# First K in fp32 by SyncE's queue, first Q by GpSimd's, two late stores by GpSimd's queue, and a redrawn order, in an attention and SiLU feed-forward kernel

## The chip, the core and the metric

The kernel runs on one core of a Trainium2 chip. The core has TensorE (matrix products, PE in the profile, with its weight loads as PEld), VectorE (DVE), ScalarE (ACT), GpSimd (POOL) and SyncE (SP), which all run at the same time and wait for each other by semaphores. SP, ACT and POOL also issue DMA transfers. The metric is the device time of one execution in microseconds (us); lower is better. The time before is a median of 384.25 us over three runs (383.94 to 386.96).

## The reference, cut to what matters

Inputs are fp32. Attention over 8 batches, 12 heads, 448 tokens and head dimension 64 gives the input of a feed-forward block with 3584 rows, width 768 and inner width 2048:

```python
scores = scale * np.matmul(q, k.transpose(0, 1, 3, 2))
scores = scores - np.max(scores, axis=-1, keepdims=True)
attn = np.exp(scores)
attn = attn / (np.sum(attn, axis=-1, keepdims=True) + 1e-09)
x = np.matmul(attn, v)            # then transposed and reshaped to (3584, 768)
h = x @ w_in
g = h * (1.0 / (1.0 + np.exp(-h)))
out = g @ w_out
```

## The kernel before, in words

**Work and tiles.** One unit of attention is one batch and a group of four heads (a "head group", three of them per batch). The first batch is cut once more into two pieces of 224 queries, so that units 0 to 2 and then 3 to 5 are the two pieces of its three head groups. All matmuls take fp16. For a unit, K and Q are loaded as [128 partitions, 14 tokens x 64], turned by VectorE (`turn_k` and `turn_q`, L411 and L422), multiplied on TensorE (`score`, L430), put through the exponential on ScalarE (`expo`, L469), summed (L510, L524), multiplied by V (L495) and scaled on VectorE into the rows of x (`norm`, L634). The feed-forward layers follow: the first (L647, and L783 for the last two pairs of batches), its SiLU (L668, L693, L829), the second (L864, and L877 for the first four output tiles), and VectorE or ScalarE collect the results in fp32 tiles called `ost`, from which `store` (L902 to L914) writes 32 rows at a time to memory.

**Loads.** Nearly all loads are DMAs of GpSimd's queue, because they turn fp32 in memory into fp16 on the way. There is one exception before the change: the first 448 columns of Q of unit 0 come in fp32 through SyncE's queue into a borrowed tile (`first_q`, L340 to L344) and ScalarE casts them to fp16 (`cast_q`, L347). The order of the other loads is a string, `LOADS`: `u` is K and Q of a unit, `v` is V, `i` a quarter of the first layer's weights, `o` a quarter of the second's.

**Stores.** Each `ost` tile of 128 x 384 leaves in four DMAs. The outputs come in 14 groups (`qd`, 0 to 13) of 256 rows, four tiles to a group. All four DMAs of a tile go through SyncE's queue, except in groups 12 and 13, where two of the four go through ScalarE's queue. Group 13 ends with tile (0, 1) and then tile (0, 0), of which VectorE copies one half and ScalarE the other (L929, L930).

**Order.** The order on every engine is not written by hand. When the program is built, a planner (`Order`, `Op`, and the loop at the end of the function) plays the work through with assumed costs and due times and emits the instructions in the order that comes out. Its constants (`NEAR`, `LATE`, `WHOLE`, the `_B` biases, `TURN`, `SOON`, `HOLD`, `DMA_PAUSES`, `FIRST_Q`) decide which of two ready pieces goes first. Where the planner sees TensorE without work in the first part, it inserts matmuls of a zero tile (`run_zeros`, L1815) that keep the engine running; the first of these blocks has at least 5120 columns. In the second half TensorE uses two ways of placing a product: whole 128 x 128 weights, or four strips of 32 columns side by side (`strips`). Changing between these and the four row strips of the scores is called a switch below.

**The end.** After its last instruction each engine executes a DRAIN and takes part in a barrier (L1922), after SyncE has waited for the landing of every DMA.

Of the kernel before, what the change touches and what calls it, by code (L numbers as in the profile page):

```python
# [9 lines left out]
FP16 = mybir.dt.float16  # L10
# [8 lines left out]
HOP = 0.10  # L19
DMA_ROW = 0.004  # L20
DMA_RATE = 13400.0
FIRST_Q = 3.5
DMA_PAUSES = ((0.0, 0.4), (4.0, 1.35), (15.5, 0.9), (21.0, 0.7), (48.5, 0.8), (65.0, 0.8))
LANES = 8
LANE = 0.28
FETCH = 5.6
# [9 lines left out]
def act(n):  # L36
    return n * 0.000824 + 0.177
# [61 lines left out]
class Order:  # L99


    def __init__(self, shy, nice):
# [3 lines left out]
        self.pool = []  # L106
        self.dma_free, self.loads, self.pauses = 0.0, [], list(DMA_PAUSES)
        self.pe_n, self.fetched = 0, 0.0
# [112 lines left out]
def kernel(  # L221
# [9 lines left out]
    nc = tc.nc  # L231

    B, NH, S, D = q.shape
# [3 lines left out]
    NG = NH // HG  # L237
    TPP = S // 32
# [9 lines left out]
    NT = 2 * S // 128  # L248
    OH = DM // 2
    NRK, NRQ = 3, 4  # L250
# [3 lines left out]
    EAGER = 1  # L254
    PAIRS = (B - 4, B - 2)
    LAST = {B - 4: range(DFF // 256), B - 2: range(DFF // 256)}
    NEAR = 0.1
    LATE = -2.0
    COLD = 8.5
    FIRST = 40  # L260
    WHOLE = 7
    TANH_B = -1
    GATE_B = -6
    ADD_B = 1
    SUM_B = -3
    COPY_B = -1
    READ_B = -2
    PAIR_B = -2
    SILU_B = -2
    HOLD = 0  # L270
    UNFOLDED = (2,)
    NICE = 0
    TILED = 3
    JOIN = 0
    STRIPS = 60.0
    LOADS = "u0 u1 u2 v0 u4 u3 i0 i3 u5 i2 u6 o0 v3 i1 u7 o1 u8 o2 v4 v5 o3"
    TURN = 8
    LOOK = 1
    SOON = -5
    KEEP = 0  # L280
    NBD = 3
    SHY = 0.5
# [10 lines left out]
    sb = ctx.enter_context(tc.tile_pool(name="sb", bufs=1))  # L293
# [11 lines left out]
    ones, half = cols[:, 16:48], (cols[:, 32:64], cols[:, 0:32])  # L305
# [16 lines left out]
    rawk, rawq, KT, QT, VT, E, T, acc, rdn_t, xT, g_t, ost_t = ({} for _ in range(12))  # L322
    sT_t, inv_t, q_tile, rdn_0 = {}, {}, {}, {}
    pS_t = {}

    def group_of(src, b, hg):
        return src[b, HG * hg : HG * (hg + 1)].rearrange("h (i g) d -> (h i) (g d)", g=TPP)
# [6 lines left out]
    def stage(name):  # L334
        t = sb.tile([128, HG, S], FP16, name=name, tag="T", bufs=NT_)
        return t.rearrange("p h s -> p (h s)").bitcast(FP32)

    first_in = {}

    def first_q():  # L340
        first_in["q"] = stage("first_q")[:, 0 : D * units[0][3]]
        nc.sync.dma_start(out=first_in["q"], in_=group_of(q, 0, 0)[:, 0 : D * units[0][3]])
        q_tile[(0, 0)] = sb.tile([128, TPP * D], FP16, name="rq_0_0", tag="rq", bufs=NRQ)
        rawq[0] = q_tile[(0, 0)][:, 0 : D * units[0][3]]  # L344

    def cast_q():
        nc.scalar.copy(out=rawq[0], in_=first_in["q"])  # L347

    def load_q(n):
        b, hg, g0, g1 = units[n]  # L350
        if (b, hg) not in q_tile:
            q_tile[(b, hg)] = sb.tile(
                [128, TPP * D], FP16, name=f"rq_{b}_{hg}", tag="rq", bufs=NRQ
            )
        rawq[n] = q_tile[(b, hg)][:, D * g0 : D * g1]
        nc.gpsimd.dma_start(out=rawq[n], in_=group_of(q, b, hg)[:, D * g0 : D * g1])
# [545 lines left out]
    def store(qd, i, j):  # L902
        u, t = divmod(2 * qd + i, NT)
        for w in range(4):
            r, col = divmod(128 * t + 32 * w, S)
            b = 2 * u + r
            dst = out[b * S : (b + 1) * S, OH * j : OH * (j + 1)].rearrange(
                "(i g) m -> g i m", g=TPP
            )

            eng = nc.scalar if w % 2 and 4 * qd + 8 >= NT * B else nc.sync
            eng.dma_start(
                out=dst[col // 32], in_=ost_t[(qd, i, j)][32 * w : 32 * (w + 1), :]
            )  # L914
# [37 lines left out]
    units = []  # L952
# [5 lines left out]
    od = Order(SHY, NICE)  # L958
    FOUR, TWO = (0, 1, 2, 3), (4, 5)
    four_ring, two_ring, m_ring, e_ring = Ring(1), Ring(1), Ring(0, (6, 7)), Ring(NE)  # L960
    rk_ring, rq_ring, v_ring = Ring(NRK), Ring(NRQ), Ring(NV)
    kt_ring, t_ring = Ring(3), Ring(NT_)
    ld_k, ld_q, ld_v, ld_win, ld_wout, wout_rows = {}, {}, {}, {}, [], []
# [7 lines left out]
    def plan_q(n):  # L971
        g0, g1 = units[n][2:]
        ring = rq_ring if g0 == 0 else None
        ld_q[n] = od.load(128, 2 * D * (g1 - g0), lambda: load_q(n), ring)
# [24 lines left out]
    NB0 = NG * len(PIECES)  # L999
    def plan_first():  # L1000
        t_ring.take()
        rq_ring.take()
        q_in = Op("SP", 0.0, first_q)
        od.emit(q_in.emit)
        q_in.done = FIRST_Q
        ld_q[0] = od.add(
            Op("ACT", act(D * units[0][3]), cast_q, [q_in], -4, tail=0.25, then=t_ring.give)
        )

    def plan(what):  # L1010
        kind, at = what[0], int(what[1:])
        if kind == "u":
            b, hg = units[at][:2]
            if at < NG or b:
                plan_k(b, hg)
            if at:
                plan_q(at)
            else:
                plan_first()
        elif kind == "v":  # L1020
            plan_v(at // NG, at % NG, NG if at == 0 else at % NG + 1)
        elif kind == "i":
            plan_w_in(DFF // 4 * at, DFF // 4 * (at + 1))
        else:
            plan_w_out(NFF // 4 * at, NFF // 4 * (at + 1))

    rest = LOADS.split()
    for n in range(NB0 + NG, NU):
        rest += [f"u{n}", f"v{n - NG}"]
    for what in rest:  # L1030
        plan(what)
# [10 lines left out]
    def plan_turn(n):  # L1042
        b, hg, g0, g1 = units[n]
        if (b, hg) not in kt_op:
            if not kt_ring.can(1, od.now):
# [3 lines left out]
                Op(  # L1049
                    "DVE", 0.77, lambda: turn_k(b, hg), ld_k[(b, hg)], TURN, then=rk_ring.give  # L1050
                )
            )
        qt_op[n] = od.add(
            Op("DVE", 0.155 + (g1 - g0) / 30.0, lambda: turn_q(n), [ld_q[n]], TURN)
        )
# [15 lines left out]
    def queue_ffn1(b, g0, g1):  # L1071
# [6 lines left out]
        for fs in turns:  # L1078

            def run(fs=fs):  # L1080
# [4 lines left out]
                for i, f in enumerate(fs):  # L1085
# [24 lines left out]
                    [th],  # L1110
                    GATE_B,
                    then=m_ring.giver(bank),
# [99 lines left out]
    def queue_pair_f(pb, f, xs):  # L1212
# [10 lines left out]

        def read(name, eng, fn, deps, then=None, bias=PAIR_B):
            busy = act(S) + 0.04 if eng == "ACT" else S / 960.0 + 0.155
# [144 lines left out]
    def plan_sums():  # L1370
# [12 lines left out]
        for m in (5, 6, 7, 3):  # L1383
            sg_op[(qd, m)] = []
            n = HF if qd < WHOLE else HF // 2
            for f0 in range(0, HF, n):
# [110 lines left out]
    def moe_ready():  # L1497

        soon, held = None, 0
        if av_data["at"] is not None and av_data["at"] <= od.now + HOLD:  # L1500
            held = len(av_seq[0][0]) if av_seq[0][1] else 1
# [183 lines left out]
    def part_at(ns, part):  # L1685
# [9 lines left out]
        for n in ns:  # L1695
# [134 lines left out]
    while True:  # L1830
        plan_turns(qk_seq[0][0][0] + 3 if qk_seq else NU)
        for ns, _, _ in qk_seq[:LOOK]:
            for op in [kt_op.get(units[n][:2]) for n in ns] + [qt_op.get(n) for n in ns]:
                if op is not None:
                    op.bias = SOON
        plan_adds()
# [3 lines left out]
        if od.free["PE"] <= od.now:  # L1840
# [86 lines left out]
```

## Time and profile before

| | before |
|---|---|
| median of three runs | 384.25 us (383.94 to 386.96) |
| the profiled execution's own time | 384.07 us |
| its span, first to last instruction | 382.3 us |
| TensorE busy | 375.4 us, 98% of the span |
| VectorE, ScalarE, GpSimd busy | 296.3, 243.2, 87.5 us |
| granted TensorE clock | 1.000 |
| first product of real data starts | 6.71 us after the span's start |
| zero matmuls on TensorE (L1815) | 44 |
| last product starts, last output copy starts (ScalarE) | 377.8 us, 378.58 us |

A profile is one execution seen by the hardware profiler. "Busy" on TensorE includes the zero matmuls, and the ends of matmuls are modelled. The span leaves out 1.77 us of the execution's own time (384.07 less 382.3), which lie around it. The chain of waits goes back from the last instruction to what released each step. A releaser is inferred, and where its own work had long been done, it was another.

### The profile page before, as it was taken

How to read it: one execution, taken by the hardware profiler on the slowest of the kernel's cores; microseconds unless marked ns; L12 is line 12 of the kernel's file. 1: busy time of each engine (PE TensorE's matmuls, PEld its weight loads, DVE VectorE, ACT ScalarE, POOL GpSimd, SP SyncE). 2: the span in 40 equal slices, each digit the busy share in tenths (PEclk: the TensorE clock that was granted, in tenths of full speed). 3: DMA queues.
4: the chain of work that ended last, by engine and by line, in shares of the span. 5: the costliest groups of instructions: out<-in, count | busy, mean ns of one | idle time of the engine just before them, and what ended most of it. 6: DMA issues, size and time to landing. Idle time of an engine off the chain costs nothing.

```text
span 382.3 us, 12926 instructions
## 1 busy us (share of the span) xinstructions
PE 375.4 (98%) x5528; PEld 197.9 (52%) x5528; DVE 296.3 (77%) x549; ACT 243.2 (64%) x378; POOL 87.5 (23%) x158
## 2 busy tenths in 40 slices
PE   8999999999999999999999999999999999999995
PEld 3667665444444444445444445555556655556663
DVE  3566676998979988897988789898899557777652
ACT  4988894788977488976487868128770138871010
POOL 7745354603306064233153200000000000000000
PEclk9999999999999999999999999999999999999999
DMA  8999999852829493729292500320002330001333
GB/s 136 199 206 205 209 151 196 147 94 26 123 50 133 104 159 47 121 43 157 70 184 38 76 9 19 79 69 0 2 0 58 94 99 2 0 2 45 103 102 83
DMA packets 37225, 34.77 MB, mean 91 GB/s; under 512 B 11696, under 2 KB 37168, under 8 KB 37168
## 3 DMA queue, kind: packets, MB, share of 16 engines
q0 software_dynamic: 26272, 22.70, 39.9%
q1 hardware_dynamic: 10128, 10.47, 10.2%
q10 hardware_dynamic: 768, 0.79, 0.8%
q8 instruction: 43, 0.70, 0.8%
q14 instruction: 14, 0.11, 0.1%
HBM read 45.61 MB, written 11.01 MB: 148 GB/s over the span
## 4 chain that ended last, share of the span: by engine, by line
PE 95%; DMA 2%; DVE 1%; ACT 1%; issue 0%; ACTq 0%; POOLq 0%
PE P L864 31%; PE P L647 20%; PE P L783 17%; PE P L430 11%; PE P L495 10%; PE P L877 3%; PE P L510 2%; DMA rk<-in_k_dram 1%; PE P L1815 1%; ACT E L469 1%; PE P L524 1%; DMA out_dram<-ost 0%; DVE xT L634 0%; DVE KT L411 0%; DVE G L693 0%
## 5 line engine op out<-in xcount | busy, mean ns | idle before, releaser
L469 ACT ACTIVATE E<-P 128x448 f16<-128x448 f32 (+6 forms) x168 | 151.2, 936 | 46.4 <-PE P L430 45.0
L647 PE MATMUL P<-xT,w_in_t 128*32 128x448 f16 (+1 forms) x1344 | 82.2, 340 | 0.0
L376 POOL DMA_DIRECT2D V<-in_v_dram x84 | 46.2, 565 | 91.0 <-PE P L495 77.1
L647 PEld LDWEIGHTS <-w_in_t 128*32 128x32 f16 (+1 forms) x1344 | 45.5, 97 | 33.9 <-issue 14.5
L864 PEld LDWEIGHTS <-G 128*32 128x32 f16 (+1 forms) x976 | 39.3, 97 | 29.2 <-issue 6.5
L430 PE MATMUL P<-rq,KT 32*128 32x448 f16 (+4 forms) x864 | 50.9, 340 | 1.0 <-DVE KT L411 0.6
L693 DVE SCALAR_TENSOR_TENSOR G<-G,P 128x448 f16<-128x448 f16 x64 | 38.6, 609 | 12.3 <-ACT G L668 11.4
L864 PEld LDWEIGHTS <-S 128*32 128x32 f16 (+1 forms) x720 | 30.8, 97 | 22.0 <-issue 3.8
L864 PE MATMUL P<-w_out_t,S 128*32 128x384 f16 (+1 forms) x472 | 39.1, 327 | 0.0
L864 PE MATMUL P<-D,G 128*32 128x384 f16 (+1 forms) x496 | 38.8, 327 | 0.0
L668 ACT ACTIVATE G<-P 128x448 f16<-128x448 f32 x64 | 35.0, 549 | 2.2 <-PE P L647 1.3
L864 PE MATMUL P<-w_out_t,G 128*32 128x384 f16 (+1 forms) x480 | 35.9, 327 | 0.0
L495 PE MATMUL P<-E,V 128*32 128x448 f16 (+2 forms) x672 | 34.3, 355 | 0.5 <-DVE xT L634 0.5
L917 DVE TENSOR_TENSOR ost<-P,u 128x384 f32<-128x384 f32 x39 | 21.5, 550 | 15.6 <-PE P L864 9.0
L783 PE MATMUL P<-sx,tw 128*128 128x448 f16 x144 | 29.9, 352 | 0.0
L634 DVE SCALAR_TENSOR_TENSOR xT<-P,R 128x448 f16<-128x448 f32 x42 | 24.3, 617 | 6.3 <-PE P L495 3.2
L430 PEld LDWEIGHTS <-KT 32*128 32x128 f16 (+2 forms) x864 | 14.4, 98 | 27.7 <-issue 23.4
L783 PEld LDWEIGHTS <-tw 128*128 128x128 f16 x192 | 18.8, 98 | 17.5
L495 PEld LDWEIGHTS <-V 128*32 128x32 f16 (+2 forms) x672 | 14.8, 95 | 18.5 <-issue 10.5
L480 DVE TENSOR_TENSOR T<-T,E 128x1792 f16<-128x1792 f16 x20 | 21.5, 1077 | 1.3 <-ACT E L469 1.2
L569 DVE STREAM_TRANSPOSE R<-P 128x448 f32<-128x448 f32 (+1 forms) x17 | 10.8, 636 | 15.1 <-PE P L510 7.4
L480 DVE TENSOR_TENSOR T<-E,E 128x1792 f16<-128x1792 f16 x20 | 21.6, 1080 | 0.1
(83 smaller groups left out, 439.6 us busy)
## 6 DMA issues: line engine op xcount, KB each, us to landing
out_dram<-ost SPq DMA_DIRECT2D x208, 48.0 KB, 1.6
rk<-in_k_dram POOLq DMA_DIRECT2D x24, 224.0 KB, 5.3
rq<-in_q_dram POOLq DMA_DIRECT2D x21, 224.0 KB, 5.8
w_in_t<-in_moe_w_in_dram POOLq DMA_DIRECT2D x12, 256.0 KB, 8.5
w_out_t<-in_moe_w_out_dram POOLq DMA_DIRECT2D x4, 768.0 KB, 10.4
V<-in_v_dram POOLq DMA_DIRECT2D x43, 64.0 KB, 4.2
V<-in_v_dram POOLq DMA_DIRECT2D x40, 48.0 KB, 4.5
out_dram<-ost ACTq DMA_DIRECT2D x16, 48.0 KB, 1.8
```

Source lines behind the costliest of these rows:

```text
L376: nc.gpsimd.dma_start(out=VT[(b, hg0)][32 * x : 32 * (x + 1), :, 0:count, :], in_=v[b, hs].rearrange("h (i g) d -> i h g d", g=TPP)[:, :, ...
L430: nc.tensor.matmul(out=P[p0 : p0 + 32 * (x1 - x0), pS[h], at : at + nq], lhsT=KT[(b, hg)][32 * h : 32 * (h + 1), c, x0:x1, :, e], rhs=QT[n ...
L469: nc.scalar.activation(out=E[(n, w)][0:kr, h0:h1, 0:nk], in_=P[0:kr, bank : bank + h1 - h0, 0:nk], func=AF.Exp, scale=attn_scale,)
L480: nc.vector.tensor_tensor(out=T[n], in0=T[n] if step else E[(n, 0)], in1=E[(n, step + 1)], op=ALU.add,)
L495: nc.tensor.matmul(out=a[32 * h : 32 * (h + 1), 0:nq], lhsT=w, rhs=e[k0:k1, h, at : at + nq], start=start, stop=stop, skip_group_check=True,)
L634: nc.vector.scalar_tensor_tensor(out=xc(b, cc)[:, 32 * g0 : 32 * g1], in0=acc[(n, part)][:, 0:nq], scalar=0.5, in1=rdn_t[n].rearrange("p g ...
L647: nc.tensor.matmul(out=h_t[(b, f, t0)][m0:m1, 0 : t1 - t0], lhsT=w_in_t[:, cc, 128 * f + m0 : 128 * f + m1], rhs=xc(b, cc)[:, t0:t1], star ...
L668: nc.scalar.activation(out=g, in_=h, func=AF.Tanh)
L693: nc.vector.scalar_tensor_tensor(out=g, in0=g, scalar=1.0, in1=h, op0=ALU.add, op1=ALU.mult)
L783: nc.tensor.matmul(out=pp_t[(*key, PBANK[m])], lhsT=w[:, c, :], rhs=xc(pb + x[0], 3 * x[1] + c) if isinstance(x, tuple) else sx_t[(pb, x)] ...
L864: nc.tensor.matmul(out=pr_t[(qd, BANK[m])][m0:m1, 0:OH], lhsT=w[:, f, m0:m1], rhs=W_[m][:, f, :], start=(f == 0 and BANK[m] == m), stop=(f ...
L917: nc.vector.tensor_tensor(out=out, in0=a, in1=b, op=op)
```

## The change

The first K takes the place of the first Q. `first_k` loads K of unit 0, 128 x 896 in fp32, through SyncE's queue; `cast_k` turns its first 448 columns to fp16 on VectorE and the other 448 on ScalarE. The first half of Q of unit 0 is now the first load of GpSimd's queue, cast by the DMA as all others. In group 13, the two stores of the output tile (0, 1), the last but one, that ScalarE's queue issued are issued by GpSimd's queue. The planner's constants and the string of loads are other ones, so that the order on every engine is drawn anew. The sums that VectorE makes for the second layer are whole instead of halved for groups 7 to 9 (`WHOLE`).

```diff
-FIRST_Q = 3.5
-DMA_PAUSES = ((0.0, 0.4), (4.0, 1.35), (15.5, 0.9), (21.0, 0.7), (48.5, 0.8), (65.0, 0.8))
+FIRST_K = 3.8
+DMA_PAUSES = ((0.0, 0.8), (4.0, 1.0), (15.5, 0.9), (21.0, 0.7), (48.5, 0.8), (65.0, 0.8))
...
-    NEAR = 0.1
-    LATE = -2.0
+    NEAR = 0.05
+    LATE = -1.0
...
-    WHOLE = 7
+    WHOLE = 10
     TANH_B = -1
-    GATE_B = -6
-    ADD_B = 1
+    GATE_B = -3
+    ADD_B = -2
...
-    PAIR_B = -2
+    PAIR_B = -4
...
-    HOLD = 0
+    HOLD = 0.6
...
-    LOADS = "u0 u1 u2 v0 u4 u3 i0 i3 u5 i2 u6 o0 v3 i1 u7 o1 u8 o2 v4 v5 o3"
-    TURN = 8
+    LOADS = "u0 u1 u2 v0 u3 u4 u5 i2 i3 u6 i0 u7 o0 v3 i1 o1 u8 o2 v4 v5 o3"
+    TURN = 20
...
-    SOON = -5
+    SOON = -2
...
-    def first_q():
-        first_in["q"] = stage("first_q")[:, 0 : D * units[0][3]]
-        nc.sync.dma_start(out=first_in["q"], in_=group_of(q, 0, 0)[:, 0 : D * units[0][3]])
-        q_tile[(0, 0)] = sb.tile([128, TPP * D], FP16, name="rq_0_0", tag="rq", bufs=NRQ)
-        rawq[0] = q_tile[(0, 0)][:, 0 : D * units[0][3]]
-
-    def cast_q():
-        nc.scalar.copy(out=rawq[0], in_=first_in["q"])
+    def first_k():
+        first_in["k"] = stage("first_k")
+        nc.sync.dma_start(out=first_in["k"], in_=group_of(k, 0, 0))
+        rawk[(0, 0)] = sb.tile([128, TPP * D], FP16, name="rk_0_0", tag="rk", bufs=NRK)
+
+    def cast_k(i):
+        half = slice(TPP * D // 2 * i, TPP * D // 2 * (i + 1))
+        copy = nc.scalar.copy if i else nc.vector.tensor_copy
+        copy(out=rawk[(0, 0)][:, half], in_=first_in["k"][:, half])
...
-            eng = nc.scalar if w % 2 and 4 * qd + 8 >= NT * B else nc.sync
+            eng = nc.sync
+            if w % 2 and 4 * qd + 8 >= NT * B:
+                eng = nc.gpsimd if 2 * qd + 2 == NT * B // 2 and (i, j) == (0, 1) else nc.scalar
```

More of the change, by code (lines that the diff above doesn't have):

```diff
@@ L1001, in plan_first @@
         t_ring.take()
[L1002 to L1008, printed above, removed]
+        rk_ring.take()
+        k_in = Op("SP", 0.0, first_k)
+        od.emit(k_in.emit)
+        k_in.done = FIRST_K
+        ld_k[(0, 0)] = [
+            od.add(Op("DVE", 0.55, lambda: cast_k(0), [k_in], -5)),
+            od.add(
+                Op(
+                    "ACT",
+                    act(TPP * D // 2),
+                    lambda: cast_k(1),
+                    [k_in],
+                    -5,
+                    tail=0.25,
+                    then=t_ring.give,
+                )
+            ),
+        ]
     def plan(what):
@@ L1013, in plan @@
             b, hg = units[at][:2]
-            if at < NG or b:
+            if at == 0:
+                plan_first()
+            elif at < NG or b:
                 plan_k(b, hg)
[L1016 to L1019, printed above, removed]
+            plan_q(at)
         elif kind == "v":
```

## The prediction, made before the changed kernel ran

> **What bounds the kernel now.** I read the page's first two parts, then busy time by stretches, then the chain of waits at the start and the timeline at the end. First the page: TensorE is busy for 98% of the span, and full in all but the first and the last slices.
>
> ```profile
> PE 375.4 (98%) x5528; PEld 197.9 (52%) x5528; DVE 296.3 (77%) x549; ACT 243.2 (64%) x378; POOL 87.5 (23%) x158
> ...
> PE   8999999999999999999999999999999999999995
> ```
>
> The stretches say where a redrawn order can win. Columns: stretch, its length, then busy time and instructions of each engine.
>
> ```profile
> 6.71:29.25 22.54, 22.08 (x462) 14.49 (x463) 13.56 (x39) 19.23 (x20) 13.05 (x22) 1.00 1.25 200
> 29.25:66.00 36.75, 36.75 (x505) 23.74 (x509) 25.78 (x50) 28.78 (x42) 17.67 (x31) 1.00 1.17 190
> 66.00:150.00 84.00, 83.53 (x1720) 38.47 (x1716) 73.84 (x122) 65.72 (x92) 27.27 (x50) 1.00 0.60 99
> 150.00:250.00 100.00, 100.00 (x2112) 47.89 (x2105) 85.88 (x142) 70.67 (x99) 24.16 (x45) 1.00 0.48 80
> 250.00:376.00 126.00, 126.00 (x725) 70.54 (x722) 94.41 (x188) 56.65 (x124) 0.00 (x0) 1.00 0.16 43
> ```
>
> From 29.25 to 376 us TensorE idles 0.47 us in all (84.00 less 83.53). The real products are the same before and after, so an order can win next to nothing there and can only lose. What is left is the start (to 29.25, with idle time and zero matmuls) and the end, after TensorE's last product at 377.8. At the start the chain is:
>
> ```profile
> 1.24 4.68 DMA rk<-in_k_dram
> 5.92 0.02 issue
> 5.95 0.72 DVE KT L411 x2
> 6.66 0.05 issue
> 6.71 0.59 PE P L430 x12
> ```
>
> The first K, through GpSimd's queue, sets the first product at 6.71; Q is ready long before (turned by 4.36). At the end VectorE finishes tile (0, 1) at 377.44 and the last tile goes VectorE, ScalarE, stores:
>
> ```profile
> 376.89 0.56 DVE L917 TENSOR_TENSOR ost<-P,u 128x384 f32<-128x384 f32 x1 [0.74 <-DMA out_dram<-ost]
> 378.19 0.36 DVE L929 COPY ost<-P 128x192 f32<-128x192 f32 x1 [0.74 <-DMA out_dram<-ost]
> 378.58 0.32 ACT L930 COPY ost<-P 128x192 f32<-128x192 f32 x1 [9.01 <-DVE ost L929]
> 378.93 0.85 ACTq L912 DMA_DIRECT2D out_dram<-ost  x2
> ```
>
> The last landing is at 381.16, SyncE has seen all of them by 381.52, and the closing barrier ends the span 0.78 later, at 382.30.
>
> **The change part by part.** I sum against the profiled execution: 384.07, which is its span of 382.30 and 1.77 around it. The median, 384.25, is 0.18 above. A difference within 1% (3.8 us) is about what a measurement of this kernel cannot tell from no change.
>
> *First K by SyncE's queue.* Removed: K's 4.68 us in GpSimd's queue and ScalarE's cast of Q (0.57). Added: one fp32 load of 448 KB, and two casts of 448 columns side by side. Moved: Q becomes the first load of GpSimd's queue. When K lands is not in the trace, so I bound it. The fp32 Q of 224 KB took 2.59 from its issue at 0.74 to 3.33, with its packets moving from 1.76 to 2.99. Twice the bytes at that rate land at 3.33 + 1.24 = 4.57. The packets themselves took 0.097 each, eight to an engine, so were they packed as densely as that K could land near 3.7. GpSimd's queue begins to move data at 2.81; were the rate halved from there, the 263 KB still to go would take 2.8 us and, with Q's 0.34 from the last packet to the landing, land at 5.95. I take 4.4, near the row for Q. Behind it stand, by the order drawn for VectorE, the cast (0.57, ScalarE's row for 448 columns; VectorE's half, an fp32 copy of 192 columns taking 0.36, is about 0.6), the turn of K (0.72), now the turn of Q too (0.41, 128x224), and 0.1 of hand-overs: 1.8 in all. The first product starts at 6.2. It cannot start before about 6.07, since the same 5632 columns of zeros stand ahead of it, and they end there. Gain 0.5 (bounds: 0.64 and a loss of 1.0).
>
> What follows does not take this back: ScalarE's first eight exponentials run 9.81 us without a pause from 7.33, so all of them move. V of the first batch lands at 13.54 and is first used at 16.07; in the new order its first use stands some 2 us earlier, at about 13.5 to 14. Ahead of V GpSimd's queue carries 112 KB less, but K in fp32 adds 448 KB for SyncE's in place of 224. At the 200 GB/s of this stretch, V lands between 0.6 earlier and 0.7 later. If later, the wait costs up to 0.7, which I keep in the range.
>
> *Fewer zeros.* Behind the first block the program before has 9856 columns of zeros, the one after 8640. At 32.52 us for 200 matmuls of 384 columns (0.42 ns a column, in the last stage) the 1216 columns are 0.5 us. This counts only if the data come when the planner expects them.
>
> *The redrawn order behind that.* Counted in both programs: switches of TensorE's mode 191 instead of 189, and 20 products whole instead of in strips. From 100 to 150 us the products, at 0.42 ns a column, fill 46.8 of the 50 us, and 38 switches share the other 3.2: at most 0.09 each, +0.2. Whole products took 0.163 (200 in 32.52), strips 0.167 (24 in 4.01): -0.1. VectorE's sums for groups 7 to 9 are cheaper but VectorE is no bound (74% busy there). +0.1 in all; stalls by mistimed loads I bound by 0 and 1.5.
>
> The start and the order sum to 0.5 + 0.5 - 0.1 = 0.9 less; I take **0.8 less** (bounds 1.2 less, 1.5 more).
>
> *Two stores by GpSimd's queue.* The output itself hides: from 377.44, plus 0.28 (GpSimd woke at 7.32 for a landing at 7.03), two issues of 0.56 end at 378.82, and the second, issued at 378.27, lands 2.2 later (the shortest for V), at 380.5, ahead of the 381.16 of the last tile. ScalarE gains nothing: its queue was free at 378.33, and its copy waits for VectorE's until 378.54. But these are GpSimd's last DMAs, and its closing DRAIN stands behind them. Before, its last DMA was a V:
>
> ```profile
> 210.10 2.22 POOL L376 DMA_DIRECT2D V<-in_v_dram  x4
> ...
> L1922 POOLq DRAIN  x3: 51/108/7494, 211.1 to 382.0; - x3
> L1922 SPq DRAIN  x3: 7/7/7, 381.5 to 381.8; - x3
> ```
>
> The longest DRAIN is the first, 211.10 to 218.60. It ended 6.28 after the last of these issues (212.32) and 3.18 after the last landing (215.42). It cost nothing, since the barrier was 163 us away; that cover is gone now. Counted from the issue it ends at 378.82 + 6.28 = 385.10, and the span 0.78 later at 385.88: +3.6. Counted from the landing, 380.5 + 3.18 = 383.7, then 384.5: +2.2. If neither holds, 0. The row is a DRAIN of this very queue behind this very kind of instruction, so I take the middle of its two readings, **+2.9**.
>
> [...]
>
> Sum: 384.07 - 0.8 + 2.9 = **386.2 us**.
>
> **The rivals.**
>
> *GpSimd's DRAIN is short here.* The one long DRAIN may have waited for a backlog: six DMAs were still moving when it began, and at the end only stores of 48 KB are under way. GpSimd's other two closing DRAINs took 0.05 and 0.11. Then the change is a small gain: 384.07 - 0.8 = 383.3 (382.9 to 384.0). It decides if the DRAIN ends before 381.5, when SyncE has seen all landings. This is the case that is not slower.
>
> *K in fp32 comes late.* For it: GpSimd's queue shares the 16 DMA engines from 2.81 on, and the DMA share of the first stretches is high. K at 5.95 puts the first product at 7.75, 1.0 later, with no zeros saved: 384.07 + 1.0 + 2.9 = 388.0; half as late, 387.3. Against it: half of K's time lies ahead of 2.81.
>
> *The new order stalls.* From 29 to 66 us loads arrive at 190 GB/s without a pause, and weights, K and Q stand in another order there. If one load comes 1 to 2 us after its turn, TensorE waits with it: 386.2 + 1.5 = 387.7.
>
> That the change does not do what it says I exclude for the queues, which the programs' orders show.
>
> **How the numbers follow.** DRAIN long and the start gains, 0.54: 386.2, own range 385.0 to 387.2. DRAIN short, 0.26: 383.3. K late, 0.11: 387.3 to 388.0. Stalls, 0.09: about 387.7, up to 389. The range 383.0 to 387.9 leaves out a part of the second case, the ends of the last two, and a DRAIN longer than read. Faster by over 1% (below 380.4) has no case: 0.01. Slower by over 1% (above 388.1) is the tail of the last two: 0.06. Within 1%: 0.93.
>
> **What would show it.** First product near 6.2 and no idle TensorE ahead of it; the cast rows at about 0.6; ScalarE's first exponential near 6.8; L1815's columns 1216 fewer; TensorE's last product near 377.0; GpSimd's DRAIN ending after SyncE's last wait, by 2 to 4 us. The prediction is wrong if that DRAIN ends with SyncE's waits, or if TensorE shows more than about 1 us of idle time between 29 and 376.

## The result and the profile after

The changed kernel takes 388.76 us, the median of eight executions (387.72 to 389.81), against 384.14 for the kernel before (median of eight, 383.93 to 387.62). The ratio is 1.010, with a 95% interval of 1.0067 to 1.0134: slower, and the interval leaves out no change. (Ratios here are not those of the two medians, which are 1.2% apart.) The forecast was 386.2 with a range of 383.0 to 387.9; the median lies 0.9 above the range. The profiled execution took 387.91 with a span of 386.1, so 1.8 lie around the span, as before.

The first two parts of the page of the changed kernel, busy time and the slices:

```profile
PE 375.0 (97%) x5463; PEld 197.5 (51%) x5463; DVE 295.2 (76%) x538; ACT 243.6 (63%) x378; POOL 88.5 (23%) x160
...
PE   7999999999999999999999999999999999999991
```

TensorE's busy time is almost the same (375.4 before). The first slice is less full than before, and the last is nearly empty, 1 where it was 5. The stretches of the changed kernel, with the same columns and borders as those shown of before, and the end added:

```profile
6.71:29.25 22.54, 22.04 (x424) 14.60 (x427) 13.59 (x38) 18.85 (x20) 12.95 (x21) 1.00 1.24 191
29.25:66.00 36.75, 36.74 (x533) 23.38 (x536) 26.07 (x51) 28.91 (x43) 17.96 (x31) 1.00 1.16 191
66.00:150.00 84.00, 83.77 (x1720) 38.40 (x1716) 74.29 (x124) 66.35 (x92) 28.44 (x53) 1.00 0.63 103
150.00:250.00 100.00, 100.00 (x2064) 48.11 (x2053) 85.06 (x140) 70.64 (x100) 22.94 (x42) 1.00 0.46 78
250.00:376.00 126.00, 125.89 (x721) 70.33 (x719) 92.91 (x175) 56.71 (x124) 0.00 (x0) 1.00 0.17 44
376.00:386.10 10.10, 2.28 (x15) 1.17 (x12) 1.19 (x3) 0.32 (x1) 1.04 (x2) 0.87 0.29 74
```

From 29.25 to 376 TensorE idles 0.35 us (0.01 + 0.23 + 0 + 0.11), 0.47 before. The long middle has no new waits. (That says nothing of how long its products take; they come up in the account of the prediction.) TensorE's last product ends at 378.28, 0.13 later than before (378.15). The span grew by 3.8, so 3.7 of it stand behind that product.

**The start.** The timeline of the changed kernel from 4 us on (start, length, engine, line, operation, and in brackets the idle time ahead and what ended it):

```profile
4.12 0.56 ACT L348 CAST rk<-first_k 128x448 f16<-128x448 f32 x1 [2.10 <-DMA first_k<-in_k_dram]
4.12 0.39 DVE L348 CAST rk<-first_k 128x448 f16<-128x448 f32 x1 [2.39 <-DMA first_k<-in_k_dram]
...
4.72 0.70 DVE L412 STREAM_TRANSPOSE KT<-rk 128x384 f32<-128x384 f32 x2 [0.20 <-ACT rk L348]
6.22 0.41 DVE L423 STREAM_TRANSPOSE rq<-rq 128x224 f32<-128x224 f32 x1 [0.80 <-DMA rq<-in_q_dram]
...
6.69 0.96 PE L431 MATMUL P<-rq,KT 32*128 32x224 f16 x24 [1.27 <-DVE rq L423]
...
7.29 0.92 ACT L470 ACTIVATE E<-P 128x896 f16<-128x896 f32 x1 [2.61 <-PE P L431]
```

K lands at 4.10 and is turned by 5.42. Then VectorE waits 0.80 for Q. The first product starts at 6.69 (6.71 before), and what ended TensorE's wait is Q's turn (L423), not K's (L412). Before, it was K's turn that ended this wait. TensorE's wait is longer than before (1.27, 0.64 before) although the first product starts at the same time, because the zeros ahead of it ended at 5.42 and not at 6.07. They are the same 5632 columns. In both traces the matmuls of 512 columns start 0.43 us apart at first; here those from 4.6 us on start 0.22 apart, before none does. The profile's record of the clock begins at 4.62 here and at 6.75 before. Ahead of it the clock is shown as 1.00, though the slow zeros there take 0.43 us for 512 columns, twice the 0.42 ns a column of the last stage. Q was issued at 1.25; fifteen of the sixteen DMA engines had their part down at 5.78, the last at 6.20.

V of the first batch has landed by 14.23, 0.7 later than before, and TensorE's weight loads wait for it:

```profile
14.27 0.70 PEld L496 LDWEIGHTS <-G 128*32 128x32 f16 x32 [0.36 <-DMA G<-in_v_dram]
```

The product behind them starts at 14.28, 0.02 after the modelled end of the zero matmuls ahead of it, so in this execution the wait cost little.

**The end.** The timeline of the changed kernel again:

```profile
377.02 0.56 DVE L920 TENSOR_TENSOR ost<-P,u 128x384 f32<-128x384 f32 x1 [0.74 <-PE P L865]
377.86 1.04 POOL L915 DMA_DIRECT2D out_dram<-ost  x2 [165.74 <-DVE ost L920]
378.32 0.36 DVE L932 COPY ost<-P 128x192 f32<-128x192 f32 x1 [0.74 <-DMA out_dram<-ost]
378.71 0.32 ACT L933 COPY ost<-P 128x192 f32<-128x192 f32 x1 [9.01 <-DVE ost L932]
379.06 0.94 ACTq L915 DMA_DIRECT2D out_dram<-ost  x2
```

Everything up to here stands as before, 0.13 later. GpSimd's two issues end at 378.90 and their data land at 379.84 and 380.20; SyncE has seen every landing by 381.54. The closing instructions of the changed kernel (shortest, median and longest in ns, then the start of the first and of the last):

```profile
L1935 POOLq DRAIN  x3: 46/108/7025, 378.3 to 385.9; - x3
L1935 SPq DRAIN  x3: 7/7/7, 381.6 to 385.6; - x3
```

GpSimd's first DRAIN begins at 378.33 and lasts 7.03, to 385.35. SyncE's, which begin at 381.6, take 7 ns. The barrier waits for GpSimd, 3.8 us in which no engine does anything.

### The profile page after: what moved, and what is told of

Same layout as the page of the kernel before. It is cut to its first block, busy times and chain, and to the rows that moved or that the text cites. A ratio compares the mean times of both kernels' runs of the same rounds, so it can differ in the third digit from the quotient of the medians.

```text
span 386.1 us, 12786 instructions
## 1 busy us (share of the span) xinstructions
PE 375.0 (97%) x5463; PEld 197.5 (51%) x5463; DVE 295.2 (76%) x538; ACT 243.6 (63%) x378; POOL 88.5 (23%) x160
## 4 chain that ended last, share of the span: by engine, by line
PE 93%; DMA 4%; DVE 1%; issue 0%; POOL 0%; ACT 0%; ACTq 0%; POOLq 0%
PE P L865 31%; PE P L648 20%; PE P L784 16%; PE P L431 10%; PE P L496 10%; PE P L878 3%; DMA rq<-in_q_dram 2%; PE P L511 2%; DMA rk<-in_k_dram 1%; PE P L525 1%; DMA out_dram<-ost 0%; PE P L1828 0%; POOL rq L357 0%; DVE xT L635 0%; DVE ost L920 0%
## 5 line engine op out<-in xcount | busy, mean ns | idle before, releaser
L694 DVE SCALAR_TENSOR_TENSOR G<-G,P 128x448 f16<-128x448 f16 x64 | 38.1, 604 | 12.8 <-ACT G L669 12.6
L915 POOL DMA_DIRECT2D out_dram<-ost x2 | 1.0, 526 | 165.7 <-DVE ost L920 165.7
```

Of the source, the lines that this page charges most:

```text
L694: nc.vector.scalar_tensor_tensor(out=g, in0=g, scalar=1.0, in1=h, op0=ALU.add, op1=ALU.mult)
```

## The experiments

Two questions stood: what the DRAIN's end counts from, and where the start's gain went. The first four kernels take the change apart.

**The changed kernel with its two stores back on ScalarE's queue.**

```diff
-                eng = nc.gpsimd if 2 * qd + 2 == NT * B // 2 and (i, j) == (0, 1) else nc.scalar
+                eng = nc.scalar
```

> The changed kernel with the two stores of tile (0, 1) back on ScalarE's queue; all else of the change stays. Theory 1 (GpSimd's closing DRAIN is the whole loss): the end of the span is bound by SyncE's waits again, GpSimd's DRAIN ends near 219, and the time is that of before within 0.4, about 384.2 us. Rival (the redrawn order or the first K costs as well, and the profiled execution hid it): it stays above 385, nearer to the 388.8 median of the changed kernel.

Measured: 383.79 (383.39 to 385.73, twelve executions) against 384.01, ratio 0.998 (0.9954 to 1.001). The long DRAIN is back in the middle, 210.26 to 218.93. It ended 3.15 after the last landing of V (215.78), as in the trace of before (3.18), but 7.48 after the last issue (6.28 before). In its trace Q landed at 5.34, the first product started at 5.83 and the last ended at 377.62. So the start and the order together are worth 0.2 us or nothing, and all that the changed kernel lost hangs on the two stores and on what varied.

**The kernel before with the two stores alone.**

```diff
             eng = nc.scalar if w % 2 and 4 * qd + 8 >= NT * B else nc.sync
+            if w % 2 and qd == 13 and (i, j) == (0, 1):
+                eng = nc.gpsimd
```

> The kernel before with only the two stores of tile (0, 1) of group 13 on GpSimd's queue; the order on TensorE is untouched. Theory 1: GpSimd's DRAIN ends about 6.4 after its last issue (378.8), at 385.2, and the span ends near 386.0; 3.7 us slower than before, 387.8, or up to 388.7 if the DRAIN varies between executions as the changed kernel's times do. Rival: the order and the first K carry the loss, and this is 384.1.

Measured: 387.89 (387.69 to 388.62) against 384.01, ratio 1.0085 (1.0059 to 1.0111): +3.9. Its closing instructions:

```profile
L1924 POOLq DRAIN  x3: 46/108/7023, 378.4 to 385.9; - x3
L1924 SPq DRAIN  x3: 7/7/7, 381.7 to 385.7; - x3
```

The last issue ended at 378.98 and the DRAIN at 385.43, 6.45 later. In the changed kernel it was 6.45 too (378.90 to 385.35).

**The same two stores two tiles earlier, and one group earlier.** These put the same instructions further from the end, to see from which point the DRAIN decides.

```diff
-            if w % 2 and qd == 13 and (i, j) == (0, 1):
+            if w % 2 and qd == 13 and (i, j) == (1, 1):
```

> The kernel before with the two stores of tile (1, 1) of group 13, two tiles earlier, on GpSimd's queue instead. VectorE ends that tile at 374.85, so GpSimd's last issue ends near 376.2. Theory 1 (a fixed 6.4 from the last issue): the DRAIN ends at 382.6, 1.1 after SyncE's last wait; about 385.2. If the DRAIN counts 3.2 from the landing (near 377.6) it ends at 380.8 and is hidden: 384.1. Rival (any late store by GpSimd costs the same, wherever it stands): 387.8.

```diff
-            if w % 2 and qd == 13 and (i, j) == (0, 1):
+            if w % 2 and qd == 12 and (i, j) == (0, 1):
```

> The kernel before with the two stores of tile (0, 1) of group 12 on GpSimd's queue. VectorE ends that tile at 370.95, GpSimd's last issue ends near 372.3. Theory 1: the DRAIN ends near 378.7, ahead of SyncE's last wait at 381.5, so it is hidden: 384.1, the same as before. Rival (late stores by GpSimd cost whatever stands behind them): 387.8.

Measured: 385.27 (384.77 to 388.38), ratio 1.0028 (0.9994 to 1.0062), for the first; 384.04 (383.43 to 386.88), ratio 0.9989 (0.9957 to 1.0021), for the second. The DRAIN of the first and then of the second:

```profile
L1924 POOLq DRAIN  x3: 46/108/7023, 375.8 to 383.3; - x3
L1924 SPq DRAIN  x3: 7/7/7, 381.6 to 383.1; - x3
```

```profile
L1924 POOLq DRAIN  x3: 46/107/7025, 371.6 to 381.9; - x3
L1924 SPq DRAIN  x3: 7/7/7, 381.3 to 381.6; - x3
```

The last issues ended at 376.35 and 372.20, the DRAINs at 382.79 and 378.64: 6.45 behind the issue again, both times. The first still ends 1.2 after SyncE is done (381.6), and its median is 1.3 above that of before; the interval of its ratio just includes no change, so it is the trace that shows the price. The second ends 2.7 before SyncE is done and costs nothing. The two point at a fixed length behind these stores, and the price is that length less the distance to the end.

**Is GpSimd itself held up, or only its DRAIN?** The changed kernel with a small memset of a spare tile on GpSimd behind its last store. It adds one instruction that computes nothing of the output (and a line that makes the tile `spare`, left out below).

```diff
             eng.dma_start(
                 out=dst[col // 32], in_=ost_t[(qd, i, j)][32 * w : 32 * (w + 1), :]
             )
+            if eng is nc.gpsimd and w == 3:
+                nc.gpsimd.memset(spare, 0.0)
```

> The changed kernel with one GpSimd memset of a spare tile of 128x16 behind its last two stores. Reading 1 (the DRAIN itself waits for the DMA's housekeeping): the memset runs at about 379.0, right behind the last issue, and the DRAIN still ends 6.4 after that issue, near 385.4. Reading 2 (GpSimd's cores are busy until then): the memset starts only near 385.3. If the memset ends the wait, the DRAIN ends by 381.5 and the span near 382.4.

Measured: 388.06. The timeline of GpSimd at the end, then the DRAIN:

```profile
377.88 1.04 POOL L917 DMA_DIRECT2D out_dram<-ost  x2 [165.76 <-DVE ost L924]
378.90 0.14 POOL L921 MEMSET spare<- 128x16 f32 x1
```

```profile
L1939 POOLq DRAIN  x3: 46/102/7135, 378.4 to 386.0; - x3
```

The memset ran right behind the issue, and the DRAIN ended at 385.51, 6.46 after the memset's end (379.04) and 6.58 after the issue's. GpSimd was free to compute; what takes 6.45 us is the DRAIN. In this one trace it counts from the last instruction, a memset. Whether a memset with no late DMA ahead of it would bring the same DRAIN was not run, and what the DRAIN waits for no trace shows: what the first reading names is the author's guess.

**The order alone.** The kernel before with the new constants and the new string of loads, but with Q in fp32 by SyncE's queue and the stores as before.

```diff
-    LOADS = "u0 u1 u2 v0 u4 u3 i0 i3 u5 i2 u6 o0 v3 i1 u7 o1 u8 o2 v4 v5 o3"
-    TURN = 8
+    LOADS = "u0 u1 u2 v0 u3 u4 u5 i2 i3 u6 i0 u7 o0 v3 i1 o1 u8 o2 v4 v5 o3"
+    TURN = 20
```

(and the other constants of the planner as in the change, `DMA_PAUSES` excepted)

> The kernel before with the change's constants and string of loads, but the first Q by SyncE's queue and the first K by GpSimd's, and the stores as before. Theory 1: the redrawn order by itself is worth nothing, 384.0 to 384.5. Rival (the new order loses what the first K wins): 384.8 or more, with TensorE's last product at 378.6 or later.

Measured: 383.73 (383.51 to 384.32) against 384.12, ratio 0.9979 (0.9959 to 0.9999): 0.4 less, which the interval only just tells from no change, with executions within 0.8 of each other. The last product ends at 377.72, 0.43 earlier than in the trace of before. But the first product already starts 0.39 earlier there (6.32 against 6.71), because K, by the same queue as before, landed at 5.53 and not at 5.92. Behind the first product the two take 371.40 and 371.44 us. So the trace does not show that the order itself gained. It is also not quite the order of the changed kernel, since the planner drew it for another start (14208 columns of zeros, 14272 in the changed kernel).

**Q first through GpSimd's queue, with no load by SyncE beside it.** The kernel before, with Q and then K of the first unit by GpSimd's queue.

```diff
-            if at < NG or b:
-                plan_k(b, hg)
-            if at:
-                plan_q(at)
-            else:
-                plan_first()
+            if at == 0:
+                plan_q(at)
+                plan_k(b, hg)
+            else:
+                if at < NG or b:
+                    plan_k(b, hg)
+                plan_q(at)
```

> The kernel before with no load by SyncE at the start: Q is the first load of GpSimd's queue, K the second, both cast by the DMA. What counts is when Q lands. If Q's late landing in the changed kernel (6.20) came from sharing the DMA engines with the fp32 K, it lands near 5.0 here; if GpSimd's first load is that slow by itself, near 6.2 again. The time is not the point: K comes later here than before, and 384.5 to 385.5 would be no surprise.

Measured: 385.24, and Q landed at 4.27 (issued at 1.24), turned at once:

```profile
4.30 0.41 DVE L422 STREAM_TRANSPOSE rq<-rq 128x224 f32<-128x224 f32 x1 [2.57 <-DMA rq<-in_q_dram]
```

The same 112 KB, first in the same queue, need 3.0 us alone and 4.9 in the changed kernel, where SyncE's 448 KB of K move at the same time: beside the profiled execution the sharing costs Q 1.9. Over the seven traces of the changed start, in which Q needs 4.1 to 5.7, that is 1.1 to 2.7, against a single trace without the sharing.

**The changed kernel once more.** Its executions spread over 2 us, and the DRAIN does not vary.

> The changed kernel once more, for the spread of GpSimd's DRAIN. Its eight executions lie between 387.7 and 389.8, and the profiled one (387.9) had a DRAIN that ended 6.45 after the last issue. If that spread is the DRAIN's, a slower profiled execution shows a longer DRAIN by as much, with TensorE's last product near 378.0 as before; if not, TensorE's last product comes later.

Measured: 390.47. The DRAIN again ended 6.45 behind the last issue (381.35 to 387.80). The 2.5 us over the profiled execution had come by TensorE's last product, at 380.73. Q had landed at 6.99 and the first product started at 7.48, with 1.74 of idle TensorE ahead. Single microseconds of this execution (after the length: busy time and instructions of each engine, then the granted clock, the DMA share and GB/s):

```profile
8.00:9.00 1.00, 1.00 (x19) 0.43 (x10) 0.89 (x3) 0.91 (x2) 0.60 (x2) 0.85 1.21 160
9.00:10.00 1.00, 1.00 (x10) 0.48 (x10) 0.11 (x1) 1.00 (x2) 0.51 (x1) 0.50 1.31 166
10.00:11.00 1.00, 1.00 (x7) 0.59 (x6) 0.46 (x1) 1.00 (x2) 0.20 (x1) 0.50 1.41 178
11.00:12.00 1.00, 1.00 (x11) 0.36 (x13) 0.54 (x3) 0.36 (x1) 1.00 (x2) 0.50 1.51 191
12.00:13.00 1.00, 1.00 (x22) 0.46 (x16) 0.00 (x0) 0.46 (x1) 1.00 (x3) 0.94 1.48 194
```

TensorE is busy throughout, but the granted clock is 0.50 for three microseconds and lower at both sides: 0.15 + 1.50 + 0.06 = 1.71 us of full speed lost, 3.4 us at half clock. In the profiled execution of the changed kernel the clock was 1.00 there. Whether the idle time ahead did this, the next two test.

**More zeros, and fewer.** The changed kernel with TensorE's first block of zeros longer by 4096 columns, and shorter by 2048; the plan is the same otherwise.

```diff
     def run_zeros(n, bank):
+        if n >= FIRST * 128:
+            n += 4096      # the other kernel: n += -2048
         for at in range(0, n, 512):
```

> The changed kernel with 4096 more columns of zeros in TensorE's first block (8 more matmuls of 512 columns) and nothing else changed. In the second execution of the changed kernel the first product came at 7.48 us instead of 6.69, and behind it the granted clock was 0.50 from 9 to 12 us; 0.79 of lateness and about 1.7 of lost clock make up the 2.45 us by which TensorE's last product came later. Theory A: the idle time of TensorE ahead of the first product sets the clock. Then with zeros until about 7.2 to 7.8 us the first product stands there in every execution, the clock is 1.00 in all of 6.71 to 29.25, the last product ends about 0.9 later than in the first execution (near 379.2), the time is 388.5 to 389.2, and the executions lie within about 0.8 of each other. Theory B: the clock fell for another reason. Then executions above 389.6 come up as before, and the spread stays near 2 us.

> The changed kernel with 2048 columns of zeros fewer in TensorE's first block (7 matmuls of 512 columns ahead of the first product instead of 11) and nothing else changed. Theory A, the idle time ahead of the first product sets the clock: the idle time grows by about 1.7 us to 2.5 or more, so the granted clock falls to about 0.5 for some 3 us behind the first product whenever Q lands, the last product ends about 1.7 later than it would, near 380.0, and the time is 389.0 to 390.5. Theory B, the clock fell for another reason: first product 5.8 to 6.7, clock 1.00, last product 377.6 to 378.4, time 387.2 to 388.1.

Measured with more zeros: 388.57 (387.97 to 389.09), ratio 1.0101 (1.0065 to 1.0138); the first product came at 8.27, later than expected, since the longer block ends there. With fewer: 388.34, one execution, between the ranges of the two theories. TensorE's timeline with more zeros, and then with fewer:

```profile
5.01 3.33 PE L1830 MATMUL P<-zeros 128*128 128x512 f16 x10
8.27 0.97 PE L431 MATMUL P<-rq,KT 32*128 32x224 f16 x24
```

```profile
6.18 0.97 PE L431 MATMUL P<-rq,KT 32*128 32x224 f16 x24 [1.82 <-DVE rq L423]
```

And the clock with fewer zeros:

```profile
7.00:8.00 1.00, 0.94 (x11) 0.53 (x9) 0.81 (x3) 1.00 (x2) 0.55 (x1) 0.89 1.16 172
8.00:9.00 1.00, 1.00 (x11) 0.61 (x8) 0.21 (x1) 1.00 (x1) 0.55 (x2) 0.50 1.10 147
9.00:10.00 1.00, 1.00 (x6) 0.42 (x4) 0.52 (x2) 1.00 (x2) 0.26 (x1) 0.50 1.26 165
10.00:11.00 1.00, 1.00 (x19) 0.44 (x16) 0.48 (x3) 0.06 (x1) 0.97 (x2) 0.50 1.41 182
11.00:12.00 1.00, 1.00 (x16) 0.41 (x10) 0.00 (x0) 0.60 (x1) 0.04 (x2) 0.90 1.49 187
```

With no idle time the clock stays at 1.00 in all of 6.71 to 29.25; with 1.82 of it the clock falls by the same 1.71 us of full speed (0.11 + 1.50 + 0.10). Idle times of 0.19, 0.47, 0.99 and 1.27 in the other traces of this start left it at 1.00; 1.74 and 1.82 did not. So the idle time does it, from somewhere between 1.27 and 1.74 us on, as far as two traces with the fall and five without can show. In both of the two the half clock begins 1.2 and 1.6 us behind the first product (near 8.70 and 7.78) and lasts 3.4 us; what sets that length no trace shows. The size of the loss was missed: with fewer zeros the last product ended at 378.72, not near 380.0. It is 0.44 later than in the profiled execution, though its first product was 0.51 earlier, so the half clock cost 0.9 to 1.0 and not 1.7. Of what was saved the trace shows 0.43: behind the first product TensorE idles 0.41 in all, 0.85 in the profiled execution. The rest was not traced. With more zeros the executions still lie 1.1 apart where 0.8 was expected.

**Q by SyncE's queue as well.** The changed kernel with its stores on ScalarE's queue and the first Q in fp32 behind K in SyncE's queue, cast by ScalarE: a version that might beat both.

```diff
+    def first_q():
+        first_in["q"] = stage("first_q")[:, 0 : D * units[0][3]]
+        nc.sync.dma_start(out=first_in["q"], in_=group_of(q, 0, 0)[:, 0 : D * units[0][3]])
+        ...
+    def cast_q():
+        nc.scalar.copy(out=rawq[0], in_=first_in["q"])
...
-            plan_q(at)
+            if at:
+                plan_q(at)
...
-                eng = nc.gpsimd if 2 * qd + 2 == NT * B // 2 and (i, j) == (0, 1) else nc.scalar
+                eng = nc.scalar
```

> The changed kernel with its two stores back on ScalarE's queue and its first Q in fp32 behind K in SyncE's queue, cast by ScalarE behind its half of K; GpSimd's queue starts with K of the next unit. Theory: what made the first product late and uncertain was Q in GpSimd's queue, which shared the DMA engines with the fp32 K and waited for the last of the sixteen. By SyncE's queue Q lands some 0.8 us behind K (its 224 KB were the difference between 3.33 and 4.10), near 4.9, is cast by 5.5 and turned by 5.95: first product near 6.0, last product near 377.7, time 383.4 to 383.8, with executions closer together than those of the variant with the stores on ScalarE alone (383.39 to 385.73). Rival: the second fp32 load delays GpSimd's loads, V lands at 14.3 or later and TensorE waits for it: 384.2 to 384.8.

Measured: 383.99 (383.16 to 385.92) against 383.97, ratio 0.9998 (0.998 to 1.0016). The median is what it was before, and the executions were no closer together. The profiled one is a quick one, 383.54: Q landed at 4.65, the first product came at 5.79, earlier than expected, and the last product ended at 377.28, 0.87 earlier than before. It shows one new wait:

```profile
13.65 0.96 PE L506 MATMUL P<-E,G 128*32 128x224 f16 x32 [0.76 <-DMA G<-in_v_dram]
```

TensorE gets to V 0.76 too soon. The rival named a wait for V, but for another reason: V was not late, it landed at 13.52 as before (13.54), and the work came to it earlier. So V caps what an earlier first product can give; its four loads stand fifth to eighth in GpSimd's queue. In this execution the wait was made up for: the planner had put in 2432 columns of zeros fewer than before, and TensorE took about as long behind the first product as before (371.49 and 371.44). Why the median did not gain is not shown.

**The last microsecond.** The stores alone cost 3.9 and the rest of the change gains 0.2 to 0.4, which makes 387.6 to 387.8; the changed kernel has 388.76. The next two ran on one chip: the changed kernel's end with Q by SyncE's queue, and the changed kernel itself. The planner drew the order of the first anew for its start, with 13056 columns of zeros and not 14272.

```diff
-                eng = nc.scalar
+                eng = nc.gpsimd if 2 * qd + 2 == NT * B // 2 and (i, j) == (0, 1) else nc.scalar
```

> The changed kernel with its stores as changed (two by GpSimd's queue) and only the start of the variant before this one: the first Q in fp32 by SyncE's queue behind K. Open is about 1 us: the stores alone cost 3.88 over before and the rest of the change, with its stores on ScalarE's queue, gains 0.2, which gives 387.7 to 387.9, but the changed kernel has a median of 388.76. Theory: that 1 us is the uncertain landing of Q through GpSimd's queue, with the half clock that follows a late first product. Then this kernel comes at 387.7 to 388.1, and its first product near 5.8. Rival: the excess has nothing to do with Q, and the long DRAIN with the new order costs it. Then 388.6 to 389.0.

> The changed kernel once more, unchanged, timed on the same chip and in turn with the kernel with Q by SyncE's queue. By the theory 388.5 to 389.0, 0.6 to 1.0 over that kernel, and some executions with a mean clock near 0.990, as the two traced executions with a late or short-covered start had. If the excess was a matter of the chip or the hour, 387.7 to 388.1, level with that kernel.

Measured: 387.24 (386.90 to 387.32), ratio 1.008 (1.0068 to 1.0092), with Q by SyncE's queue; 388.40 (387.17 to 389.29), ratio 1.0105 (1.0087 to 1.0123), for the changed kernel. The intervals overlap only from 1.0087 to 1.0092, the difference of the medians is 1.16, and the spread falls from 2.1 to 0.4. Both came out below what was expected. So that microsecond hangs on Q's way in together with the order drawn for it. By the traces the last products lie 1.79 apart (377.76 and 379.55), of which 1.22 are there at the first product and 0.60 are time in zero matmuls behind it. The half clock is not seen here: the traced execution of the changed kernel has none, and no execution of it on this chip had a mean clock under 0.993, where some near 0.990 were expected. The start with Q by SyncE's queue:

```profile
4.77 0.56 ACT L358 CAST rq<-first_q 128x448 f16<-128x448 f32 x1
...
5.37 0.41 DVE L433 STREAM_TRANSPOSE rq<-rq 128x224 f32<-128x224 f32 x1
...
5.83 0.97 PE L441 MATMUL P<-rq,KT 32*128 32x224 f16 x24 [0.20 <-DVE rq L433]
```

In the changed kernel's trace on that chip Q landed at 6.57 and the first product started at 7.06, 0.37 later than in the profiled execution. The last product was 1.27 later, though the clock was 1.00 in every stretch up to 376. A wait that was not there before tells of a part of the rest:

```profile
141.35 0.71 DVE L412 STREAM_TRANSPOSE KT<-rk 128x192 f32<-128x192 f32 x2 [1.69 <-DMA rk<-in_k_dram]
...
142.93 0.58 DVE L694 SCALAR_TENSOR_TENSOR G<-G,P 128x448 f16<-128x448 f16 x1
...
143.57 0.75 PE L648 MATMUL P<-xT,w_in_t 128*32 128x448 f16 x12 [0.62 <-DVE G L694]
```

VectorE waits 1.69 for a later K, and its next multiplication (L694), which reads a product of TensorE's and on which TensorE then waits, stands behind that turn. In the profiled execution VectorE waited 0.69 at this place and TensorE not at all:

```profile
139.90 0.70 DVE L412 STREAM_TRANSPOSE KT<-rk 128x192 f32<-128x192 f32 x2 [0.69 <-DMA rk<-in_k_dram]
```

The execution of 390.47 shows the same wait with 0.76. A late Q alone does not explain it: in the kernel with the memset Q landed at 5.78, earlier than in the profiled execution, and the wait is there with 0.30. The order on every engine is fixed when the program is built, for loads that come at one time, and an execution in which they come later can pay at more than one place.

## Why the prediction was wrong

The direction was right, and so was the cause named for it; the size was 2.6 us short of the median. By the profiled executions: the sum was -0.8 for start and order and +2.9 for the stores; measured are +0.13 by TensorE's last product and +3.7 behind it. Taken from the start of each matmul to the start of the next, the 0.13 is 0.02 less ahead of the first product, 0.27 less in zero matmuls behind it, 0.50 more in real products with their switches, and 0.08 less in idle time. The remaining 0.85 is the difference between the profiled execution and the median (387.91 and 388.76).

- **First K by SyncE's queue: the step that failed is the 6.2 for the first product.** K was well judged: landed at 4.10 (taken 4.4, bounds 3.7 to 5.95), cast in 0.56 and 0.39 (0.57 and 0.6), turned in 0.70. The step then put Q's turn right behind K's, as though Q were there. Q had been moved from the quick queue (224 KB in 2.59 before) to the slow one (112 KB in 4.9), and its landing was not priced at all, though the text lists the move. It landed at 6.20, and from 5.34 to 6.99 over seven traces of this start. Gain 0.02 in the profiled execution instead of 0.5, and a loss of 0.35 and 0.77 in two others. The lower bound of 6.07, the end of the zeros ahead, was no bound either: the same 5632 columns ended between 5.36 and 6.07, and where Q landed at 5.34 the first product started at 5.83.
- **V, 0.6 earlier to 0.7 later.** It came 0.7 later, at the far end. The products lost next to nothing by it in the profiled execution, because the first product came no earlier. Where it did come earlier, V took back 0.41, 0.76 and 0.81 in three traces; the step had such a wait in its range and not in its sum.
- **Fewer zeros, 0.5 less.** The 1216 columns fewer came (14272 in all, 15488 before), but they saved 0.27 and not 0.5. The condition named ("only if the data come when the planner expects them") was not met for Q. And idle time here is not neutral: 1.74 and 1.82 us of it brought the half clock, 1.27 did not.
- **The order, 0.1 more: too small.** The waits were as forecast, 0.35 us idle from 29.25 to 376. But the real products with their switches take 0.50 more, although switches (191 for 189) and whole products (20 more) are as counted. In the second layer, where the whole products were to save 0.1, products take 0.19 more by the traces; what makes the difference was not tested. The rival of a stalling order did not show in the profiled execution; it shows as 0.30, 0.62 and 0.76 in three other traces.
- **The stores, 2.9 more: the right DRAIN, the term too small.** The issues ended at 378.90 (forecast 378.82), the barrier took 0.79 (0.78). Of the two readings of the DRAIN the one from the issue held for the stores, with 6.45 for 6.28: +3.7 in the trace, +3.9 for the stores alone. The one from the landing fell there: the last landing was 5.15 ahead of the DRAIN's end, not 3.18. Taking the middle of two readings of one row was the mistake; the DRAIN's end kept to the landing behind V and to the issue behind the stores, and the row before could not tell the two apart. That the 6.28 came so close was luck. Behind V loads the DRAIN ended 6.2 to 7.6 after the last issue in five traces, but 3.12 to 3.19 after the last landing in all of them. So the row of before followed the landing, and the stores do not behave like it.
- **The rival of a short DRAIN** (0.26) fell. Behind V loads, with its backlog (five loads, by the trace, and not six, were issued and not landed when the DRAIN began), the end came 3.12 to 3.19 after the last landing in five traces. But without it the DRAIN was long as well (7025 ns, where SyncE's took 7).
- **The rival of a late K** had the wrong transfer: K was in time, Q was late. That the median came out within 0.8 of the 387.3 to 388.0 it gave is chance, since it added a first product 1.0 late to a DRAIN of 2.9. Its argument against itself, that half of K moves ahead of GpSimd's data, fits what came: Q took 4.9 for the 3.0 it needs alone, and K landed at 4.10, ahead of the 4.4 taken.

Of the signs named, the zeros' 1216 columns fewer, the cast on ScalarE (0.56; VectorE's took 0.39) and the DRAIN's end 2 to 4 us behind SyncE's last wait (3.8) came; the first product at 6.2 without idle time, the exponential at 6.8 (7.29) and the earlier last product did not. The chance of slower by over 1% was 0.06; the ratio lies on that line.

What stays open: the changed kernel's start with the stores on ScalarE's queue reached 383.79 on another chip, where Q landed at 5.34. Q's landing differs between executions on one chip (5.69 to 6.99 in four traces); whether it also differs by chip the traces are too few to say. With fewer zeros 0.8 of the 1.71 us of lost clock did not reach the end, and only a part of that was followed. Why the real products take longer, and why the kernel with K and Q by SyncE's queue did not gain by its median, is open too. No variant beat the kernel before by more than 0.21%; the new order without the rest (383.73) is the best of them.

## What to carry to other kernels

Before a DMA is put on GpSimd's queue near the end of a kernel, look for GpSimd's long closing DRAIN in the trace and place it behind the new last instruction: it is hidden only if that instruction is farther from the end than the DRAIN reaches (6.45 us here). A row of a DRAIN behind another kind of DMA gave no sure length here; one trace with the DMA in its new place gave it (6.45, and 6.37 to 6.45 in nine). When two loads change queues, price the landing of both; the one that goes to the slower queue, behind the bytes of the other, may be the new limit. And where a change starts the real work earlier, look at once for the next load that the work will meet.

## What the runs showed of the hardware

- **GpSimd's closing DRAIN was long behind its DMAs, and not by one rule.** Behind two stores of 48 KB it ended 6.37 to 6.45 us after the last issue in nine traces, at whatever distance from the end they stood; their data had landed 1.30 to 1.35 after the issue. With a memset behind the stores it ended 6.46 after the memset, in one trace. Behind the V loads in the middle of the program it ended 3.12 to 3.19 after the last landing and 6.2 to 7.6 after the last issue, in five traces, and was hidden.
- **TensorE's first zeros ran at two paces.** Matmuls of 512 columns started 0.43 us apart and later 0.22 apart. The change of pace came at another time in each execution (at 4.6 us in the profiled execution of the changed kernel; not by the end of the zeros in that of before), so the same 5632 columns ended between 5.36 and 6.07, while the profile shows a clock of 1.00.
- **Idle TensorE at the start cost clock.** 1.74 and 1.82 us of it brought 3.4 us of granted clock 0.50, starting some 1.2 to 1.6 us behind the first product; 1.27 us did not.
- **A load through GpSimd's queue was slowed by a neighbour's, and by its last part.** 112 KB took 3.0 us from issue to landing alone, and 4.1 to 5.7 beside 448 KB in SyncE's queue. In the profiled execution of the changed kernel the sixteenth part came 0.42 behind the fifteenth (6.20 and 5.78). The 448 KB took 3.3 to 3.4 each time, and 224 KB of Q behind them in the same queue landed at 4.65 and 4.75, 0.5 to 0.7 after K.
